# Attention and Fourier mixing on one core: 27 pairs of v loads change their issuing queue, from SyncE to ScalarE

## The chip, the cores and the metric

The kernel runs on one core of one Trainium2 chip. The metric is the device time in microseconds of one execution. A core has five engines that run side by side, each with an instruction queue of its own that is worked through in order: PE (TensorE, matrix products), DVE (VectorE), ACT (ScalarE), POOL (GpSimd) and SP (SyncE, which here only issues transfers). Transfers are issued by an instruction on one engine's queue, and the bytes are then moved by 16 DMA engines. An issue on SP is written SPq in the profile, one on ACT ACTq.

## What is computed

Top-k attention over 8 batches of 8 heads (576 rows, head size 64, the 32 largest scores of each row kept), whose output goes through a Fourier mixing, a normalisation and a two-layer network:

```python
scores = scale * np.matmul(q, k.transpose(0, 1, 3, 2))
kth = np.partition(scores, -top_k, axis=-1)[..., -top_k:-top_k + 1]
scores = np.where(scores >= kth, scores, -1e9)
attn = np.exp(scores - np.max(scores, axis=-1, keepdims=True))
attn = attn / (np.sum(attn, axis=-1, keepdims=True) + 1e-09)
out = np.matmul(attn, v)                        # (8, 8, 576, 64) -> x (8, 576, 512)
...
mixed = np.real(np.fft.fft(np.fft.fft(x, axis=1), axis=2))
u = x + mixed
un = (u - mu) / np.sqrt(var + 1e-06)
return u + np.maximum(un @ w_ch1, 0.0) @ w_ch2
```

All data are float32.

## The kernel before

**Work items.** Two heads make a pair (NPB = 4 pairs in a batch, 32 pairs), and a pair has nine items: five tiles of query rows, four of them once for each head. One step of the main loop (L1492) works on one item, so a batch is 36 steps and a pair nine. In step i the stages of several items run side by side: the scores of item i+3 (`scores`, PE, drained by ACT, L404, L375, L393), the search for the 32 largest of item i (`top_ops`, DVE, L425 and L427), the mask of item i-1 (`mask`: L448 on ACT, L451 on POOL), its exponential (`expo`, L459 on ACT), and for item i-2 the split of the weights into 16-bit halves (`plane`, two copies L472 on ACT), which SP writes to a scratch in HBM (L485, L488). `turn` (L506) reads the scratch back transposed into the tile PT, by a transposing transfer issued on SP. `attend` (L564) multiplies PT with v on PE, once for each of a pair's two chunks of rows: the first takes place a step after the transposition of the fifth item, the second after the ninth. This path through HBM is used by pairs from the second batch on, but for pairs 7 and 31; the others are transposed by PE (`transposes`).

**The mixing and the network.** Work of the batch before (`dft_tokens` L755, `dft_channels` L812 and L816, `channels_first` L881, and the network's `hidden` L966, `back` L993 and L1032, `fast` L1163) is cut into units, which the loop puts between the attention's matmuls so that PE is filled to an even level. Their results leave PSUM by ACT (L786, L833, L884, L970), in part with POOL (L839, L1108). In the first batch there is no such work; the weights of the network are converted instead.

**Order.** The order on every engine is that in which the program is written, a step after the other; nothing is rearranged. Transfers use eight completion semaphores in turn, whatever their queue, and a transfer waits until the one that had its semaphore before has landed.

**Loads.** At the end of a step the loop issues the loads of a coming pair: k in step 0 (L267, L271), q in step 5 (L240, L279), v in step 7 (L1599), all on SP. v has two tiles (L152), pair p in tile p % 2. `load_v` (L284) issues four transfers: for each of the two heads the first 512 rows (L288, 128 KB), and then, in `load_tails`, the last 64 rows (L255, 16 KB). Only the loads at the very start (L1271, L1275, L1277) are issued on ACT.

Of the kernel before, what the change touches and what calls it, by code (L numbers as in the profile page):

```python
# [73 lines left out]
def kernel(  # L74
# [9 lines left out]
    nc = tc.nc  # L84
# [11 lines left out]
    NPB = H // 2  # L96
# [129 lines left out]
    nat, qT_of, kT_of, v_of, PT, Ssb, Wk, Wp, M8, Nt = ({} for _ in range(10))  # L226
# [6 lines left out]
    def head_of(src, pair, e):  # L233
        b, hp = divmod(pair, NPB)
        return src[b, 2 * hp + e]
# [9 lines left out]
    def load_tails(dst, src, pair, queue=None, heads=(0, 1)):  # L245
        for e in heads:
            if src is q:
                for h in range(2):
                    (queue or nc.sync).dma_start(
                        out=dst[TH * h:TH * (h + 1), NF, e, :],  # L250
                        in_=head_of(src, pair, e)[HS * h + 2 * P:HS * (h + 1)],
                    )
            else:
                r0 = TAIL * e if src is v else 0
                (queue or nc.sync).dma_start(  # L255
                    out=dst[r0:r0 + TAIL, NF, e, :], in_=head_of(src, pair, e)[NF * P:S]
                )
# [26 lines left out]
    def load_v(pair):  # L284
        if pair < NPAIR:
            v_of[pair] = v_t[pair % 2]
            for e in range(2):
                nc.sync.dma_start(  # L288
                    out=v_of[pair][:, 0:NF, e, :],
                    in_=head_of(v, pair, e)[0:NF * P].rearrange("(c p) d -> p c d", p=P),  # L290
                )
            load_tails(v_of[pair], v, pair)

    def prep(n, pair, blocks=((0, NF), (NF, NC))):

# [1016 lines left out]
    for n in range(3):  # L1312
        load(n)
    load_v(0)
    load_nat("q", 1)
    for n in range(3, AHEAD):
# [123 lines left out]
    queue, waiting, pending, written, now, out_next = [], [], [], set(), [0], []  # L1440
    step_us = 6.0

    def chunk_at(i):

        for tile in (i - 4, i - 3, i - 2):
            r = tile % PER_PAIR
            if PER_BATCH <= tile < N and r in (4, 8):
                if i - tile == (4 if by_dma(tile) else 2 if tile == 2 * PER_BATCH - 1 else 3):
                    return tile // PER_PAIR, r // 8
        return None, None  # L1450
# [41 lines left out]
    while i < N + 5 or plan or queue or sums:  # L1492
# [49 lines left out]
        if short:  # L1542
            fixed += tok
            pair, r = divmod(i - 1, PER_PAIR)
# [39 lines left out]
        pair, ch = chunk_at(i)  # L1584
# [8 lines left out]
        if i < N:  # L1593
            if q_step:
                load_nat("k", pair_of + 1)
            if i % PER_PAIR == 5:
                load_nat("q", pair_of + 2)
            if i % PER_PAIR == 7:
                load_v(pair_of + 1)  # L1599
# [63 lines left out]
```

## Time and profile before

| | |
|---|---|
| median of 3 runs | 1876.23 us (1875.66 to 1876.6) |
| the profiled execution | 1876.57 us |
| its span on the core | 1874.8 us |
| mean granted clock of TensorE | 0.955 |
| SP's plain transfers of the planes, L485 and L488 | 260 issues |
| SP's transposing transfers, L506 | 130 issues, median 4.6 us from issue to landing |
| v's loads | 64 of 128 KB (3.0 us to landing) and 64 of 16 KB (2.5 us) |
| transfers in all | 249.16 MB, mean 133 GB/s |

The span is the time from the first to the last instruction of the profiled execution. "Busy" does not count issuing transfers or waiting for semaphores. In the page's slices the span is cut into 40 equal parts of some 47 us, and a digit is the busy share in tenths. The first batch ends after some 235 us; from the third batch on a batch takes about 205 us; the last batch's network runs alone from about 1703 us. In a row of the timeline the columns are the start, the duration, the engine, the line and operation, what is written and read, the number of instructions merged into the row, and in brackets the engine's idle time before it with what ended it.

### The profile page before, as it was taken

The page shows a single profiled execution, that of the slowest core. Times are in us where ns is not written, and L with a number is a line of the kernel's source. Part 1 is how long each engine was busy: PE and PEld are TensorE (multiplying, and loading weights), DVE is VectorE, ACT ScalarE, POOL GpSimd, SP SyncE. Part 2 cuts the span into 40 slices and gives each one's busy share as a digit, 9 for nine tenths or more (in the row PEclk, how much of TensorE's full clock was granted, in tenths as well). Part 3 has the DMA queues.
Part 4 walks back from the last instruction along what each step waited for, and adds up shares of the span by engine and source line. Part 5 has one row for each costly group of instructions (what it writes and reads, how often), then busy time and mean ns, then how long its engine had stood idle before and what let it go on. Part 6 is the DMA issues. An engine that isn't in the chain of part 4 may idle for free.

```text
span 1874.8 us, 26903 instructions
## 1 busy us (share of the span) xinstructions
PE 1703.8 (91%) x8134; PEld 1086.4 (58%) x8134; DVE 1583.8 (84%) x3301; ACT 1295.0 (69%) x3104; POOL 912.5 (49%) x1278
## 2 busy tenths in 40 slices
PE   5566699789899899999999999989999999999999
PEld 3344465355466555666556565666567555677677
DVE  7999989888899999999999899899999899762110
ACT  6878659577788788877787678767787678652100
POOL 4768643454746266355545465255545364341012
PEclk7777799999999999999999999999999999999999
DMA  5333016661557755586466745694566645530132
GB/s 167 104 98 109 20 46 170 168 164 26 137 146 202 187 130 136 150 209 161 123 161 180 180 114 132 155 231 127 122 162 182 172 121 143 130 111 6 51 114 69
DMA packets 516576, 249.16 MB, mean 133 GB/s; under 512 B 398288, under 2 KB 506448, under 8 KB 516432
## 3 DMA queue, kind: packets, MB, share of 16 engines
q1 hardware_dynamic: 515664, 247.23, 50.9%
q8 instruction: 65, 1.06, 0.2%
q14 instruction: 79, 0.65, 0.1%
q10 hardware_dynamic: 768, 0.21, 0.0%
HBM read 93.63 MB, written 84.74 MB: 95 GB/s over the span
## 4 chain that ended last, share of the span: by engine, by line
PE 55%; DVE 13%; ACT 10%; POOL 10%; issue 6%; DMA 4%; SPq 2%; POOLq 0%; DVEq 0%; ACTq 0%
PE hp L966 22%; PE o L564 7%; DVE wk L427 6%; DVE m L425 6%; PE sp L401 4%; PE cp L993 4%; POOL wk L451 4%; PE cw L1163 3%; PE cv L1163 3%; PE cp L1032 3%; ACT wk L448 2%; POOL fg L651 2%; PE yp L755 2%; ACT wk L472 2%; PE sp_t L371 2%
## 5 line engine op out<-in xcount | busy, mean ns | idle before, releaser
L451 POOL TENSOR_TENSOR wk<-S,wk 128x576 f32<-128x576 f32 x288 | 408.1, 1417 | 549.8 <-ACT wk L448 533.9
L425 DVE MAX8 m<-wk 128x8 f32<-128x576 f32 x864 | 626.5, 749 | 6.2
L966 PE MATMUL hp<-unT,w 128*128 128x256 f32 (+1 forms) x2048 | 529.5, 411 | 5.2 <-ACT unT L884 2.7
L966 PEld LDWEIGHTS hp<-unT,w 128*128 128x128 f32 x2048 | 382.5, 192 | 116.5 <-issue 10.7
L427 DVE MATCH_REPLACE8 wk<-m,wk 128x576 f32<-128x576 f32 x576 | 427.4, 742 | 0.0
L472 ACT COPY wk<-S 128x576 uint16<-128x576 uint16 x468 | 289.1, 668 | 0.0
L448 ACT ACTIVATE wk<-S,nt 128x576 f32<-128x576 f32 x288 | 222.9, 774 | 85.4 <-POOL nt L434 84.5
L564 PE MATMUL o<-PT,v 128*64 128x256 f32 (+3 forms) x1440 | 204.8, 430 | 37.9 <-DMA PT<-planes 19.5
L993 PE MATMUL cp<-w,hT 128*128 128x512 f32 x512 | 236.4, 602 | 0.0
L425 DVE MAX8 m<-S 128x8 f32<-128x576 f32 x288 | 213.5, 741 | 7.8 <-ACT S L375 7.8
L459 ACT ACTIVATE S<-wk,nt 128x576 f32<-128x576 f32 x234 | 184.2, 787 | 48.3 <-POOL wk L451 47.2
L427 DVE MATCH_REPLACE8 wk<-m,S 128x576 f32<-128x576 f32 x288 | 213.5, 741 | 0.0
L970 ACT ACTIVATE hT<-hp 128x320 f32<-128x320 f32 (+1 forms) x256 | 103.9, 412 | 156.3 <-PE hp L966 155.2
L401 PE MATMUL sp<-kT,qT 64*128 64x512 f32 (+1 forms) x528 | 170.7, 676 | 24.2 <-ACT kT L318 9.4
L564 PEld LDWEIGHTS o<-PT,v 128*64 128x64 f32 x1440 | 117.9, 158 | 114.9 <-issue 37.0
L404 ACT COPY S<-sp 128x512 f32<-128x512 f32 (+1 forms) x264 | 141.6, 586 | 24.4 <-PE sp L401 23.3
L993 PEld LDWEIGHTS cp<-w,hT 128*128 128x128 f32 x512 | 93.4, 193 | 91.4 <-issue 91.0
L1108 POOL TENSOR_TENSOR hT<-hT 128x512 f32<-128x512 f32 x64 | 81.6, 1277 | 106.5 <-ACT hT L970 91.5
L434 POOL TENSOR_TENSOR nt<-m,cc 128x2 f32<-128x2 f32 x288 | 59.1, 205 | 126.2 <-DVE m L425 122.5
L371 PEld LDWEIGHTS sp_t<-kt,qT 128*128 128x128 f32 x320 | 51.3, 196 | 108.9 <-issue 70.0
L1163 PE MATMUL cw<-w,hT 128*128 128x256 f32 x448 | 105.0, 381 | 1.5 <-POOL hT L1108 0.9
L527 PE MATMUL tpP<-ident,wk 128*128 128x128 f32 x216 | 40.8, 320 | 61.1 <-ACT wk L459 36.1
(160 smaller groups left out, 2174.3 us busy)
## 6 DMA issues: line engine op xcount, KB each, us to landing
planes<-wk SPq DMA_DIRECT2D x208, 288.0 KB, 2.7
w<-w_parts SPq DMA_DIRECT2D x82, 512.0 KB, 4.7
space<-in_moe_w_ch_dram SPq DMA_DIRECT2D x32, 512.0 KB, 3.7
nat<-in_q_dram SPq DMA_DIRECT2D x128, 64.0 KB, 2.7
v<-in_v_dram SPq DMA_DIRECT2D x64, 128.0 KB, 3.0
out_dram<-x SPq DMA_DIRECT2D x32, 256.0 KB, 2.7
nat<-in_k_dram SPq DMA_DIRECT2D x62, 128.0 KB, 3.0
planes<-wk SPq DMA_DIRECT2D x52, 144.0 KB, 2.6
```

Source lines behind the costliest of these rows:

```text
L401: nc.tensor.matmul(sp[r], lhsT=qT[hd, q_cols], rhs=kT[hd, :], start=True, stop=True)
L404: nc.scalar.copy(out=s_t[r, keys], in_=sp[r])
L425: ops.append(lambda src=src, m8=m8: nc.vector.max(out=m8, in_=src))
L427: ops.append(lambda src=src, m8=m8: nc.vector.match_replace(w, m8, src, NEG))
L448: nc.scalar.activation(out=w, in_=Ssb[i], func=AF.Relu, scale=-FAR, bias=Nt[i][:, 1:2])
L451: nc.gpsimd.tensor_tensor(out=w, in0=Ssb[i], in1=w, op=ALU.subtract)
L459: nc.scalar.activation(out=Ssb[i] if by_dma(i) else w, in_=w, func=AF.Exp, bias=Nt.pop(i)[:, 0:1], accum_out=den_t[pair % 3][:, c:c + 1],)
L472: nc.scalar.copy(out=words[:, half, :], in_=src[:, half, :])
L564: nc.tensor.matmul(o[D * e:D * (e + 1), c0:c1], lhsT=vv[:, c, e, :], rhs=pt[:, NF if c == NF else (NF + 1) * e + c, c0:c1], start=(c == 0) ...
L966: nc.tensor.matmul(hp[:, 0:w], lhsT=w1[:, dt, P * it:P * (it + 1)], rhs=unT[:, dt, 0:w], start=(dt == 0), stop=(dt == NDT - 1),)
L993: nc.tensor.matmul(cp, lhsT=hT[:, it, P * n:P * (n + 1)], rhs=w2[:, it, :], start=(it == 0), stop=(it == NIT - 1),)
L1163: nc.tensor.matmul(dst, lhsT=h()[a][:, kc, :], rhs=rhs_of(kc), start=start and kc == 0, stop=kc == NK - 1, skip_group_check=True,)
```

## The change

`load_v` chooses the queue by the number of the pair: SP for pairs 0 to 4, ACT for pairs 5 to 31. The place of the call in the program stays the same, the end of step 7, and so do the tiles, the sizes and the order of the four transfers.

```diff
     def load_v(pair):
         if pair < NPAIR:
             v_of[pair] = v_t[pair % 2]
+            queue = nc.sync if pair <= NPB else nc.scalar
             for e in range(2):
-                nc.sync.dma_start(
+                queue.dma_start(
                     out=v_of[pair][:, 0:NF, e, :],
                     in_=head_of(v, pair, e)[0:NF * P].rearrange("(c p) d -> p c d", p=P),
                 )
-            load_tails(v_of[pair], v, pair)
+            load_tails(v_of[pair], v, pair, queue)
```

`load_tails` had the argument for the queue already; without it, it uses SP. Pair 4 is the first of the second batch; as its load is issued in the first batch, it stays on SP.

## The prediction

> **What bounds the kernel now.** I read the page's busy times and slices first, then the windows view by batch, then the rows of v's loads, the waits, and the timeline around each load.
>
> ```profile
> PE 1703.8 (91%) x8134; PEld 1086.4 (58%) x8134; DVE 1583.8 (84%) x3301; ACT 1295.0 (69%) x3104; POOL 912.5 (49%) x1278
> ...
> PE   5566699789899899999999999989999999999999
> ...
> ACT  6878659577788788877787678767787678652100
> ```
>
> From about 480 us on PE is full and ACT is not. The windows view of two whole batches (PE, PEld, DVE, ACT, POOL busy, then clock, DMA share, GB/s) says how full:
>
> ```profile
> 896.00:1101.00 205.00, 199.03 (x962) 125.44 (x959) 192.02 (x398) 157.86 (x377) 105.39 (x157) 0.98 0.62 159
> ...
> 1311.00:1516.00 205.00, 198.68 (x964) 125.01 (x963) 191.46 (x397) 156.87 (x373) 104.63 (x154) 0.99 0.63 158
> ```
>
> PE 97% (199.03 / 205), DVE 94%, ACT 77%. So the price of anything put on ACT is what it makes PE wait. That is read place by place, since ACT drains every PSUM bank PE fills, in one fixed order.
>
> **What moves.** Pairs 5 to 31 are affected: 27 bursts of four issues (two of L288, two of L255), 108 in all. The same bytes go to the same tiles. The tile view of v gives the issue times on SP (min/median/max ns):
>
> ```profile
> L288 SPq DMA_DIRECT2D v<-in_v_dram x64: 419/570/1085, 8.0 to 1614.8; - x64
> L255 SPq DMA_DIRECT2D v<-in_v_dram x64: 513/595/794, 9.2 to 1616.0; - x64
> ```
>
> Four medians make 2 x 0.570 + 2 x 0.595 = 2.33 us. From the start of the first issue to the end of the fourth, the 27 bursts take a median of 2.53 us on SP, and I use that. In total 27 x 2.53 = 68 us leave SP and enter ACT's instruction order, where nothing behind a burst is dispatched until it is issued. Does an issue on ACT cost the same? The only rows are the first microseconds, when both queues issue at once:
>
> ```profile
> 0.74 0.97 SPq L240 DMA_DIRECT2D nat<-in_q_dram  x2
> 1.75 0.98 SPq L240 DMA_DIRECT2D kn<-in_k_dram  x2
> ```
> ```profile
> 0.74 0.41 ACTq L1271 DMA_DIRECT2D ident<-c_id  x1
> 1.19 1.09 ACTq L240 DMA_DIRECT2D kn<-in_k_dram  x2
> 2.32 0.54 ACTq L255 DMA_DIRECT2D kn<-in_k_dram  x1
> ```
>
> ACT takes 0.41 to 0.55 us an issue, SP 0.49, side by side. So the bounds of a burst on ACT are 4 x 0.41 = 1.64 us and, from the longest SP rows, 2 x 1.085 + 2 x 0.794 = 3.76 us. 2.53 is nearest to both queues' usual rows.
>
> **The waits that come with it.** Each load waits for the landing of an earlier transfer, normally the one eight back in the program's order, because eight completion semaphores go round. On ACT that could block the engine behind SP's queue. I compared, for each of the 108, the landing in this trace with the end of the ACT instruction ahead of the burst. Nearly all had landed 0.2 to 21 us before; the exceptions are the bursts at 1035.0 us (its fourth load's transposition lands at that moment) and at 1450.8 us (1.0 us later, but a fourth load starts some 1.9 us after the first). The wait for v's buffer is long over: its last reader ran four steps earlier. I cost these waits at nothing.
>
> **What lies behind a burst, and who waits.** Behind it on ACT stand the next step's mask (L448), the two half-word copies (L472), the score copies (L404, L375, L393) and the PSUM drains. L451 on POOL, SP's L485, and PE wait for these. I walked each place on the timeline: ACT becomes 2.53 us late; each idle gap of ACT takes off its length (not where it waited for POOL's L451, which is late too); at every matmul that waits for an ACT result, the stall is what is left of the lateness minus the matmul's own margin (its start minus that result's end). Two ends of the scale, first one of the two worst, the burst at 738.0 us, which goes after the first row:
>
> ```profile
> 737.88 0.20 ACT L459 ACTIVATION_READ_ACCUMULATOR S<-wk,nt 128x1 f32 x1
> 737.97 0.77 ACT L448 ACTIVATE wk<-S,nt 128x576 f32<-128x576 f32 x1
> ...
> 750.39 1.52 ACT L393 COPY S<-sp 64x256 f32<-64x256 f32 x4
> ...
> 751.19 2.84 PE L401 MATMUL sp<-kT,qT 64*128 64x512 f32 x4 [1.73 <-ACT S L393]
> ```
>
> ACT has only 0.2 us of gaps in these 13 us, and PE already waits for L393, with 0.05 us margin: it loses 2.3 us. The other end, at 1303.7:
>
> ```profile
> 1304.19 0.78 ACT L448 ACTIVATE wk<-S,nt 128x576 f32<-128x576 f32 x1 [0.48 <-POOL nt L434]
> ...
> 1314.26 0.43 ACT L786 COPY y<-yp 128x290 f32<-128x290 f32 x1 [2.53 <-PE yp L755]
> ```
>
> 0.48 + 2.53 us of gaps swallow it, and no matmul in between has a margin under 2.05 us. The cover here is ACT's wait for PE and DVE; without it, 2.5 us would be lost. Over the 27 places the stalls are: pair 7 2.4, pair 14 2.3, pair 17 1.3, pair 8 1.1, pairs 6, 22, 26 and 30 about 0.8 each, pairs 9 and 18 about 0.6 each, the other 17 none. Sum 11.7 us (rounding aside). With 1.64 us a burst the same walk gives 3.6 us, with 3.76 us it gives 31.2.
>
> Smaller terms. POOL is late with ACT, but of the matmuls that wait for POOL within 14 us of a burst only yp at 498 to 503 us has a margin under 2.5 us, and that stall is the same time as pair 9's above: nothing more. Transfers: v on a queue of its own shares the 16 engines with the transposition that SP has just issued, instead of standing behind it, and for ten pairs the first attend starts within 0.2 us of that landing. A burst is 2 x 128 + 2 x 16 = 288 KB, 1.8 us at the window's 159 GB/s if all of it stood in the way: 0 to 18 us, and as the transposition is ahead I take 2. Against these, PE time lost is not lost twice where PE later waits for something else: it idles some 53 us between 480 and 1700 us in this trace. I take 3 off (bounds 0 and all 11.7). Sum: 11.7 + 2 - 3, about +11 us on the profiled execution's 1876.57 us, which is 0.3 us over the median: 1887.
>
> **What SP gets back.**
>
> ```profile
> 738.47 1.22 SPq L288 DMA_DIRECT2D v<-in_v_dram  x2
> 739.74 1.33 SPq L255 DMA_DIRECT2D v<-in_v_dram  x2
> 741.17 0.60 SPq L485 DMA_DIRECT2D planes<-wk  x1
> ```
>
> At 14 of 27 bursts the next SP transfer starts within 0.11 us of the last v issue, so v held it up. But that L485 waits for L472 copies which now stand behind the burst on ACT. Here they end at 739.9 and would end at 742.4, later than the 741.17 at which L485 starts now. I credit nothing.
>
> [...]
>
> **The rivals.** That the moved loads would not move is no rival: the built program has all 108 on ACT.
> - *Forecast (0.56).* +11 us, 1887. Its own range is the walk's two ends with the small terms, 1880 to 1908.
> - *Hidden (0.20).* A burst counts 1.64 us, because its issue overlaps the ACT work ahead, and later PE waits take back what is left of the 3.6: 0 to +3 us, about 1878. For: 17 of 27 places lose nothing even at 2.53. Against: the row ahead of a burst is mostly the accumulator read of 0.2 us, which covers little.
> - *Issues collide (0.10).* A burst meets one of SP's transposition issues (L506, median 2.48 us) and waits it out: 2.53 + 2.48 = 5.0 us late at each place, for which the same walk gives about 59 us, 1936. For: one of them is often in progress within 2 us of a burst. Against: the side-by-side rows.
> - *SP's queue was the brake (0.14), the other side.* Planes and transpositions go out up to 2.53 us sooner and PE stops waiting for PT. The tile view of o has PE's idle time ahead of attend (us, times):
>
> ```profile
>   DMA PT<-planes: 22.8, 7
> ```
>
> All of it gone would be 1854; half of it, 11 us, gives 1865. It decides if PE's second attend of a pair, whose transpositions SP issues after v, is the one that waits. For: the 14 places. Against: of the second attends only one (615.9 us, 4.7 us) starts at its landing, the others have 0.7 us or more; the first attend's transpositions are issued ahead of v.
>
> **How the numbers follow.** What a measurement of this kernel can tell from no change is about 0.2%, 3.75 us: 1872.5 to 1880. The hidden case is "same", 0.20; the brake case is "faster", 0.14; the forecast and the collision are "slower", 0.56 + 0.10 = 0.66. The range 1870 to 1910 holds the forecast's and the hidden case's; it leaves out most of the brake case (0.09) and the collision (0.10).
>
> **What the new profile would show.** Right: 27 groups of four ACTq rows for v, 2.3 to 2.8 us each, the fourth with no gap for a wait; more time in PE's waits for ACT (sp <- L393 is 8.1 us between 480 and 1703 us now) at the places named, most at 751 us and after the bursts of pairs 22, 26 and 30; SP's L485 after the old v slot no earlier than now by more than a few tenths. Wrong: single ACTq rows of 2 us or more (collision, or a blocked semaphore); PE waits for ACT unchanged (hidden); the 22.8 us of PT waits clearly smaller (brake). The forecast falls also if the first attends start 1 us or more later after the burst than their margin allows, since I took nearly nothing for the shared transfer engines.

## The result, and the profile after

The changed kernel takes 1886.78 us (median of four runs, 1883.47 to 1888.17), the kernel before beside it 1875.96 (1875.66 to 1876.6). The ratio is 1.0055, 95% interval 1.0037 to 1.0072: slower by some 10 us, 7 to 14 by the interval. The profiled execution took 1888.17 us, with a span of 1886.3 us and a mean granted clock of 0.948 (0.955 before).

The page's busy times and slices of the changed kernel:

```profile
PE 1715.3 (91%) x8134; PEld 1093.6 (58%) x8134; DVE 1584.0 (84%) x3301; ACT 1293.2 (69%) x3104; POOL 911.6 (48%) x1278
...
PE   6567699789899999999999999999999899999999
...
ACT  6878658666787777777787678767787678652100
```

PE still bounds the kernel and is as full as before. It executes the same 8134 matmuls, but is busy 11.5 us longer (1715.3 against 1703.8), while its idle time over the whole span, the span less the busy time, is 171.0 us in both. So either matmuls became slower, or "busy" holds something that isn't work. This is taken up below.

The windows of two whole batches, the same two as before (the columns are the window's length, then busy us of PE, PEld, DVE, ACT, POOL, then clock, DMA share and GB/s):

```profile
905.00:1110.00 205.00, 197.87 (x963) 125.03 (x960) 191.74 (x398) 156.62 (x376) 104.55 (x156) 0.98 0.62 158
1320.00:1526.00 206.00, 197.50 (x962) 125.02 (x962) 190.83 (x396) 155.50 (x374) 103.76 (x155) 0.98 0.62 158
```

One batch is as long as before, the other 1.7 us longer by the lag at its two ends. The lag of a matmul is how much later than in the kernel before it starts. It goes up and down in steps: +4.9 us at 464 us, +2.7 at 643, +8.6 at 844, +10.2 at 1046, +8.7 at 1171, +11.6 at 1601. Some of what is lost is given back where PE has another wait anyway.

v's loads in the tile view (min/median/max ns):

```profile
L289 ACTq DMA_DIRECT2D v<-in_v_dram x54: 368/466/722, 283.8 to 1630.2; - x54
L255 ACTq DMA_DIRECT2D v<-in_v_dram x54: 472/607/1517, 285.0 to 1631.4; - x54
```

All 108 are on ACT, and a row costs about what it cost on SP (medians 466 and 607 ns, 570 and 595 there). A burst, from the start of the first row to the end of the fourth, has a median of 2.21 us (2.14 to 3.05). The timeline of ACT around one burst (columns as in the timelines above):

```profile
1311.83 0.38 ACT L971 ACTIVATE hT<-hp 128x256 f32<-128x256 f32 x1 [1.20 <-PE hp L967]
1311.84 0.93 ACTq L289 DMA_DIRECT2D v<-in_v_dram  x2
1312.81 1.17 ACTq L255 DMA_DIRECT2D v<-in_v_dram  x2
1314.09 0.78 ACT L449 ACTIVATE wk<-S,nt 128x576 f32<-128x576 f32 x1 [1.87 <-DMA v<-in_v_dram]
```

The first issue starts at 1311.84, while L971 runs until 1312.21: here ACT's queue issues a transfer 0.37 us before the instruction ahead of it ends. So the burst of 2.14 us leaves a hole of 1.87 us, in which ACT computes nothing. Over the 27 bursts the hole has a median of 1.82 us (0.89 to 2.59), 45.0 us in all. That is the number that the prediction's 2.53 stood for. The holes of 0.89 to 1.05 us stand where several ACT instructions ahead of the burst still ran while it was issued (the loads of pairs 5, 14, 18, 22, 26 and 30); there the first issue starts some 1.4 us before the last of them ends.

PE's waits from 480 us to the last attend, first before, then after (us in total, times, longest):

```profile
PE o L564 <- DMA PT<-planes: 10.4, 3, 4.7
PE o L564 <- DVE m L425: 9.3, 3, 4.3
PE sp L401 <- ACT S L393: 8.1, 6, 2.1
PE sp L401 <- ACT kT L318: 5.1, 5, 1.2
PE o L564 <- DVE x L1121: 4.5, 2, 2.8
```
```profile
PE o L565 <- DMA PT<-planes: 13.5, 5, 6.5
PE o L565 <- DVE m L426: 9.6, 3, 4.7
PE sp L402 <- ACT S L394: 9.0, 6, 2.6
PE sp L402 <- ACT kT L319: 5.9, 5, 1.4
...
PE o L565 <- DMA v<-in_v_dram: 3.5, 2, 3.2
PE o L565 <- DVE wk L428: 3.1, 1, 3.1
```

The waits for ACT grew by 0.9 and 0.8 us only. The waits of the attends (the rows with o; some are put down to a DVE instruction, though an attend reads nothing of DVE's, only PT and v, which transfers bring) went from 10.4 + 9.3 + 4.5 = 24.2 us to 13.5 + 9.6 + 3.5 + 3.1 = 29.7 us.

A load on ACT did not wait for an issue on SP here. The burst for pair 6 goes out within one of SP's transposing issues, which lasts 7.82 us, and its four rows are as short as elsewhere (timeline of ACT, then of SP):

```profile
329.07 1.13 ACTq L289 DMA_DIRECT2D v<-in_v_dram  x2
...
330.25 1.36 ACTq L255 DMA_DIRECT2D v<-in_v_dram  x2
```
```profile
324.21 7.82 SPq L507 DMA_TRANSPOSE PT<-planes  x1
```

SP, relieved of 68 us of issues, waits for ACT instead. In the waits of its queue the row of the planes goes from the first of these lines (before) to the second (after):

```profile
SPq L485 <- ACT wk L472: 352.1, 112, 15.4
```
```profile
SPq L486 <- ACT wk L473: 427.8, 129, 15.4
```

**Where 11.5 us of busy time come from.** One attend shows it: pair 23's first. Timeline of PE before, then after:

```profile
1249.52 0.49 PE L371 MATMUL sp_t<-kt,qT 128*128 128x128 f32 x2
1251.63 2.91 PE L564 MATMUL o<-PT,v 128*64 128x320 f32 x20 [1.62 <-DVE x L1121]
```
```profile
1258.26 0.49 PE L372 MATMUL sp_t<-kt,qT 128*128 128x128 f32 x2
1261.94 4.34 PE L565 MATMUL o<-PT,v 128*64 128x320 f32 x20 [3.19 <-DMA v<-in_v_dram]
```

PE waits 1.62 us before and 3.19 after; the same 20 matmuls then take 2.91 and 4.34 us. (The brackets name DVE and a load of v, but the v that this attend reads had landed by 1210.15 us. What lands last is the pair's third transposition, at 1261.69 us, 8.39 us after its issue began; v's first issue follows that by 1.50 us. Before, v's followed by 4.73 us, and the transposition took 6.74 us.) The windows view gives the clock over those matmuls, before and after (the last three numbers: granted clock, DMA share, GB/s):

```profile
1252.00:1256.00 4.00, 4.00 (x27) 2.67 (x24) 3.97 (x10) 2.50 (x7) 1.61 (x2) 1.00 0.91 248
```
```profile
1261.90:1264.90 3.00, 2.96 (x12) 1.65 (x14) 2.97 (x8) 1.03 (x2) 1.58 (x2) 0.51 0.73 241
```

Behind the longer wait the clock is halved for 3.4 us. The wait cost 1.57 us more, the slow attend another 1.43 us. (Here both are given back: some 10 us later the kernel before waits 2.4 us for a weight, the changed one doesn't, and the lag is 8.7 us again, as it was ahead of the attend.) Adding up the clock's records from 240 us on, the profiled execution of the kernel before has 64.9 us at half clock in 13 stretches, that of the changed one 92.2 in 19, each 3.4 or 6.8 us long. If work goes at half speed in them, 27.3 us more are worth up to 13.7 us of PE's time, an estimate from the granted share (0.51 in the window above).

That the idle time over the whole span is the same is chance. The window from 240 us, before the first moved load, to the end, in the kernel before, then in the changed one:

```profile
240.00:1874.80 1634.80, 1551.53 (x7389) 994.36 (x7385) 1357.68 (x2826) 1109.92 (x2672) 750.71 (x1105) 0.98 0.54 138
```
```profile
240.00:1886.30 1646.30, 1558.10 (x7377) 998.28 (x7373) 1358.18 (x2821) 1108.20 (x2672) 749.10 (x1105) 0.97 0.53 137
```

Up to 240 us, where nothing has moved yet, PE is idle 4.9 us less in the changed kernel's execution (82.8 against 87.7), and from there on 5.0 us more (88.2 against 83.3). From the first moved load to the end the same matmuls take 13.1 us longer, 5.0 of them idle and 8.2 busy. So in these two executions the stalls are the smaller part of the loss, and PE running slower behind them is the larger.

How long a wait must be for the clock to be halved behind it isn't shown: 2.09 us at 1158.2 us in the kernel before was followed by 6.8 us at half clock, while 2.84 us at 838.6 was followed by none.

### The profile page after: what moved, and what is told of

It reads as the page before. It is cut to its first block, busy times and chain, and to the rows that moved or that the text cites. A ratio compares the mean times of both kernels' runs of the same rounds, so it can differ in the third digit from the quotient of the medians.

```text
span 1886.3 us, 26881 instructions
## 1 busy us (share of the span) xinstructions
PE 1715.3 (91%) x8134; PEld 1093.6 (58%) x8134; DVE 1584.0 (84%) x3301; ACT 1293.2 (69%) x3104; POOL 911.6 (48%) x1278
## 4 chain that ended last, share of the span: by engine, by line
PE 56%; ACT 10%; DVE 10%; POOL 10%; issue 5%; DMA 5%; SPq 2%; ACTq 1%; POOLq 0%; DVEq 0%
PE hp L967 22%; PE o L565 7%; DVE m L426 4%; PE sp L402 4%; DVE wk L428 4%; PE cp L994 4%; POOL wk L452 4%; PE cw L1164 3%; PE cp L1033 3%; PE cv L1164 3%; ACT wk L449 2%; PE yp L756 2%; ACT wk L473 2%; POOL fg L652 2%; DMA planes<-wk 2%
## 5 line engine op out<-in xcount | busy, mean ns | idle before, releaser
L565 PE MATMUL o<-PT,v 128*64 128x256 f32 (+3 forms) x1440 | 210.6, 439 | 44.2 <-DMA PT<-planes 25.1
L971 ACT ACTIVATE hT<-hp 128x320 f32<-128x320 f32 (+1 forms) x256 | 103.4, 411 | 150.0 <-PE hp L967 149.0
L402 PE MATMUL sp<-kT,qT 64*128 64x512 f32 (+1 forms) x528 | 174.7, 692 | 24.6 <-ACT S L394 9.2
L405 ACT COPY S<-sp 128x512 f32<-128x512 f32 (+1 forms) x264 | 141.4, 584 | 24.0 <-PE sp L402 21.3
L435 POOL TENSOR_TENSOR nt<-m,cc 128x2 f32<-128x2 f32 x288 | 58.3, 202 | 87.5 <-DVE m L426 82.8
L402 PEld LDWEIGHTS sp<-kT,qT 64*128 64x128 f32 (+1 forms) x528 | 47.5, 196 | 83.8 <-issue 31.0
```

What stands on the lines that cost most here:

```text
L402: nc.tensor.matmul(sp[r], lhsT=qT[hd, q_cols], rhs=kT[hd, :], start=True, stop=True)
L405: nc.scalar.copy(out=s_t[r, keys], in_=sp[r])
L565: nc.tensor.matmul(o[D * e:D * (e + 1), c0:c1], lhsT=vv[:, c, e, :], rhs=pt[:, NF if c == NF else (NF + 1) * e + c, c0:c1], start=(c == 0) ...
```

## The experiments

Each ratio is against the kernel before, run beside it on the same chip, with its 95% interval; 0.1% is 1.9 us. A single profiled execution stands some us beside its kernel's median, so that numbers from one trace show places, and the ratios show prices.

### Hold and load taken apart

What is asked first is whether the hold of ACT costs the 10 us, or v's way through another queue. Four kernels: v's loads left out, ACT held without moving v, both, and half of the burst moved.

`no_v`, v's loads of pairs 5 to 31 left out:

```diff
     def load_v(pair):
         if pair < NPAIR:
             v_of[pair] = v_t[pair % 2]
+            if pair > NPB:
+                return
```

> The loads of v for pairs 5 to 31 are left out (attend multiplies with the v of pairs 3 and 4), so neither SP nor ACT issues them. Theory 'hold' (the change costs because ACT is held while it issues; SP gets nothing back): as the kernel before, 0.998 to 1.001, since 68 us of issues on SP lie beside other work. Rival 'brake' (SP's issues of v hold up planes and transpositions): faster, 0.994 or less. Rival 'queue' (the loss comes from v's transfers running beside the transpositions on a queue of their own): 0.998 to 1.001 as well.

Measured: 1870.82 us against 1877.44, ratio 0.9968 (0.9956 to 0.9979).

`sp_hold`, the loads on SP as before, and ACT held by four copies at the same places. The copies stood on ACT for 1.90 us at every place (51 us in all), next to the burst's hole of 1.82 (45 us in all):

```diff
+    held = const.tile([P, 344], U16, name="held", tag="held")
+
+    def hold():
+        for _ in range(4):
+            nc.scalar.copy(out=held, in_=w1[:, 0, 0:172].bitcast(U16))
...
             if i % PER_PAIR == 7:
                 load_v(pair_of + 1)
+                if NPB < pair_of + 1 < NPAIR:
+                    hold()
```

> v stays on SP as in the kernel before; at the place where the change put the burst on ACT, ACT does four copies of 128x344 16-bit words onto a scratch instead, about 1.9 us, for the same 27 pairs. Theory 'hold': slower like the change, 1.004 to 1.007, with the granted clock at half for some 20 to 30 us more than before after 240 us. Rival 'queue': 0.999 to 1.001, since no transfer moved. Rival 'semaphores' (SP's later transfers wait for the landing of a v load that ACT issues late): 0.999 to 1.001.

Measured: 1884.03 us, ratio 1.0033 (1.0021 to 1.0045).

`no_v_hold`, both edits together:

> Both: v's loads for pairs 5 to 31 are left out and ACT is held for about 1.9 us at their 27 places. Theory 'hold': the same as sp_hold within 0.2%, 1.003 to 1.007. Rival 'queue': as no_v, 0.998 to 1.001. If SP's relief and ACT's hold both counted, this would lie clearly under sp_hold.

Measured: 1876.13 us, ratio 0.9995 (0.9980 to 1.0010).

`half`, the two 128 KB loads of a burst on ACT, the two tails on SP:

```diff
-            load_tails(v_of[pair], v, pair, queue)
+            load_tails(v_of[pair], v, pair)
```

> The change with one part undone: the two loads of 128 KB are issued on ACT, the two of 16 KB stay on SP. 256 of a burst's 288 KB still run on ACT's queue, but ACT is held for some 0.4 us (0.9 us of issues less the 0.4 to 0.8 us by which a burst starts before the ACT instruction ahead of it ends). Theory 'hold': the walk gives under 1 us, so 0.999 to 1.002. Rival 'queue': most of the loss stays, 1.004 to 1.006.

Measured: 1883.31 us, ratio 1.0026 (1.0014 to 1.0038).

None of the four met the ranges of theory 'hold': `no_v` is faster than it allows, `no_v_hold` lies in its rival's range, `sp_hold` lies just under it, and `half` lies between it and its rival.

What follows: at step 7 the hold costs 0.33% with v on SP, and 0.9995 - 0.9968 = 0.27% with no v at all, so it is a price of its own, 5 to 6 us, wherever v goes. The change costs 0.55%, so 0.22% are left for v's way, with an uncertainty of some 0.2% from the two intervals. `half` shows better that such a second part exists: its two issues mostly run under the instruction ahead and leave ACT without work for 0.32 us on average while they go out (8.7 us in all, against 40.6 us for the change counted the same way), and yet it loses 0.26%. At the price of `sp_hold`, 6.2 us for 51, 8.7 us would be worth 1.1 us, 0.06%. The tile view of o in `half` has these rows of PE's and ACT's idle time ahead of the attends:

```profile
  DVE m L426: 29.5, 10
  DMA PT<-planes: 27.7, 8
  DVE wk L428: 18.2, 7
```

Before, the rows that answer were 21.3, 22.8 and 1.4 us (and 13.3 for another DVE row, which `half` doesn't have): 58.8 us then, 75.4 in `half`. From 480 us on the waits of PE ahead of the attends are 24.2 us before, 23.3 in `sp_hold`, 29.6 in `half` and 29.7 in the changed kernel. So in these traces the attends wait longer where v goes out on ACT, and not where ACT is only held. Whether these waits are the loss is another question, to which the last group of runs below has an answer.

### One step later

`act_s8` keeps the changed kernel's queue and moves the place from step 7 to step 8; `sp_s8` moves the place alone, on SP.

```diff
-            if i % PER_PAIR == 7:
+            if i % PER_PAIR == (7 if pair_of < NPB else 8):
                 load_v(pair_of + 1)
```

> The changed kernel with v's burst on ACT's queue one step later from the second batch on: step 8 of a pair instead of 7. At step 7 the pair's third transposition (t = 4) has just been issued and chunk 0's attend of the same pair waits for it; at step 8 that attend stands ahead of the burst and no transposition is issued in the step. Theory 'two parts' (ACT held about 0.3%; v on a queue of its own slows the transposition beside it, and the attends of pairs 10, 15, 19, 23 and 27 wait longer for it, about 0.25%): the second part goes, ratio 1.002 to 1.004, 1880 to 1885 us at a before of 1877, and the lag at those five attends against the kernel before grows by less than 0.5 us each. Rival 'the queue's semaphores or the issues alone cost it, wherever they stand': ratio 1.005 to 1.007 as in the changed kernel. Rival 'the hold alone': 1.005 too, as the hold is the same, or another number if step 8 takes a hold better or worse.

Measured: 1878.65 us against 1877.73, ratio 1.0002 (0.9986 to 1.0018). Neither number expected: the loss is gone, the hold's part too. The lag at the five attends named, counted from the matmul ahead of each, grows by 0.10, 2.17, 1.43, 0.41 and 2.59 us, where less than 0.5 was expected (in the changed kernel by 1.22, 0.94, 0.78, 1.56 and 2.25). So these attends start as late as in the changed kernel, and yet the kernel is no slower.

> The kernel before with v's four loads still on SP's queue but at step 8 of a pair instead of 7 from the second batch on. Theory 'v's transfer beside the third transposition costs the before kernel something too' (leaving v out gained 0.3%): ratio 0.997 to 0.999. Rival 'on SP the loads queue behind the transposition anyway and what leaving v out gained is SP's issue time, which is the same at step 8': 0.999 to 1.002.

Measured: 1875.18 us, ratio 0.9990 (0.9978 to 1.0002). It lies between the two expectations, and isn't told from no change.

`hold_s8` is `sp_hold` with the four copies one step later and v at step 7 on SP:

```diff
-                if NPB < pair_of + 1 < NPAIR:
-                    hold()
+            if i % PER_PAIR == 8 and NPB < pair_of + 1 < NPAIR:
+                hold()
```

> The kernel before with v on SP's queue at step 7, as it was, and ACT held at the end of step 8 instead of step 7 by the same four copies (some 1.9 us, 27 places). The step 7 hold cost 0.33%, and the burst on ACT at step 8 (v moved there too) cost 0.02%. Theory 'a hold costs by the slack of the transpositions and copies behind it, about the same at both steps' (walking the slack of the before trace with 1.84 us at each place gives 5.0 us at step 7 and 6.4 us at step 8): ratio 1.002 to 1.004, and v's later place gained what hid it. Rival 'step 8 has the slack for it': 0.999 to 1.001, and the change would have cost nothing one step later for that reason.

Measured: 1880.40 us against 1878.62, ratio 1.0013 (1.0003 to 1.0024), between the two theories. The same 1.90 us on ACT cost 0.33% at step 7 and 0.13% at step 8. Together with v's place, -0.10%, that is +0.03%, and `act_s8` has +0.02%; but each of these three is known to 0.1 or 0.16% only, so that they neither show nor exclude a part for the queue as such at step 8. The walk of the slack, which gave 5.0 us for step 7 (measured 6.2) and 6.4 for step 8 (measured 2.5), doesn't foresee the difference between steps.

The copies also stand for more than v's burst at step 8. There more ACT instructions stand just ahead of the burst, and the queue issues under all of them (timeline of ACT in `act_s8`, the burst for pair 23):

```profile
1202.28 1.07 ACT L405 COPY S<-sp 128x512 f32<-128x512 f32 x2
1202.78 1.04 ACTq L289 DMA_DIRECT2D v<-in_v_dram  x2
...
1203.86 0.69 ACTq L255 DMA_DIRECT2D v<-in_v_dram  x1
1204.12 0.23 ACT L460 ACTIVATION_READ_ACCUMULATOR S<-wk,nt 128x1 f32 x1
1204.59 0.61 ACTq L255 DMA_DIRECT2D v<-in_v_dram  x1
1205.25 0.78 ACT L449 ACTIVATE wk<-S,nt 128x576 f32<-128x576 f32 x1 [0.90 <-POOL nt L435]
```

The burst begins 1.57 us before the last of them ends, and the hole is 0.90 us, which is also the median of the 27 places at step 8 (34.8 us in all), against 1.82 at step 7 (45.0 us in all). So the change costs nothing that can be measured one step later, ACT is held for less there at most places, and a hold of the same length costs less there too; how much each of these gives isn't shown.

`act_s8` also has in full what the prediction looked for in the changed kernel, issues on ACT that wait for another transfer (timeline of ACT):

```profile
1040.31 0.52 ACTq L289 DMA_DIRECT2D v<-in_v_dram  x1
...
1041.31 0.22 ACT L460 ACTIVATION_READ_ACCUMULATOR S<-wk,nt 128x1 f32 x1
1041.51 2.04 ACTq L255 DMA_DIRECT2D v<-in_v_dram  x2
1043.60 0.77 ACT L449 ACTIVATE wk<-S,nt 128x576 f32<-128x576 f32 x1 [2.07 <-DMA w<-w_parts]
```

The third issue starts 0.02 us after one weight load lands (1041.49), the fourth 0.02 us after the next (1043.06), and ACT stands for 2.07 us. A wait of this kind happens at three of the 27 places (pairs 16, 20 and 28 of the loads). In the changed kernel, where the same loads go out at step 7, it happens once: the fourth issue of pair 28's burst waits 0.53 us, to 1460.54, for a transposition that lands at 1460.52.

### Which of the 27 places cost

A theory from the two traces: SP issues a pair's third transposition only after its planes have landed (in all, its queue waits for planes 107 times ahead of L506 in the kernel before, 204.3 us); ACT doesn't wait for that. In the kernel before, v's first issue always comes 2.0 us or more after the start of that transposition's issue. In the changed kernel it comes ahead of it at seven places (pairs 5, 10, 15, 17, 19, 27 and 29). Pair 19, timeline of SP in the changed kernel (v goes out on ACT from 1043.62 to 1046.02):

```profile
1042.51 1.23 SPq L489 DMA_DIRECT2D planes<-wk  x2
1043.84 1.16 SPq L910 DMA_DIRECT2D w<-w_parts  x2
1046.25 1.31 SPq L507 DMA_TRANSPOSE PT<-planes  x1
```

The transposition that chunk 0's attend waits for starts 2.6 us after v's first issue; the planes ahead of it take 3.05 us to land (2.48 at the same place before), the transposition 5.88 (5.58 before). The three kernels that were made to try this put v on ACT at the eight places alone where it goes first or the transposition landed latest (`only8`: the loads of pairs 6, 11, 16, 18, 20, 24, 28 and 30), at the 19 others alone (`other19`), and on SP but ahead of the transposition at all 27 (`sp_early`).

```diff
-            queue = nc.sync if pair <= NPB else nc.scalar
+            queue = nc.scalar if pair in (6, 11, 16, 18, 20, 24, 28, 30) else nc.sync
```

> The kernel before with v on ACT's queue in 8 of the 27 places alone: where, in the trace of the changed kernel, the burst was issued before the third transposition of the pair it stands in (pairs 5, 10, 15, 17, 19, 27, 29: 0.1 to 7.3 us before it) or that transposition landed latest (pair 23: 8.4 us). Theory 'overtaking' (SP waits for the planes' landing before it issues that transposition, ACT doesn't wait, so v's 295 KB go first and chunk 0's attend, which TensorE already waits for in these pairs, gets its PT later): most of the loss is in these 8, ratio 1.003 to 1.005 (5 to 9 us), 0.6 us or more of lag at the attends of pairs 10, 15, 19, 23 and 27. Rival 'the loss is spread evenly, by ACT's hold at every place': 8/27 of 0.55%, ratio 1.001 to 1.002.

Measured: 1881.26 us against 1877.83, ratio 1.0013 (0.9998 to 1.0028).

> The complement: v on ACT's queue in the 19 other places, on SP's in those 8. Theory 'overtaking': ratio 1.000 to 1.0025 (0 to 5 us, what ACT's hold costs where the transposition is first). Rival 'spread evenly': 19/27 of 0.55%, ratio 1.003 to 1.0045.

Measured: 1886.29 us, ratio 1.0043 (1.0030 to 1.0057).

`sp_early`:

```diff
+        if i < N and i % PER_PAIR == 7 and pair_of >= NPB:
+            load_v(pair_of + 1)
         turn(i - 3)
...
-            if i % PER_PAIR == 7:
+            if i % PER_PAIR == 7 and pair_of < NPB:
                 load_v(pair_of + 1)
```

> The kernel before with v's four loads still on SP's queue, but issued at the start of step 7, ahead of the third transposition instead of behind it (from the second batch on). ACT isn't held at all and no second queue is used. Theory 'overtaking': v's bytes are again ahead of the transposition, at all 27 places, and SP's 2.1 us of issues too where the planes have landed by then: slower, ratio 1.002 to 1.006, with lag at the attends of pairs 10, 15, 19, 23 and 27. Rival 'a queue of its own on ACT is what costs, not the order': 0.999 to 1.001.

Measured: 1881.44 us, ratio 1.0015 (1.0001 to 1.0029).

The theory that the loss sits in those eight places falls: they cost 0.13%, the 19 others 0.43%, and the sum, 0.56%, is the whole change. Per place that is as good as even (0.016% and 0.023%). Order by itself isn't free, though: `sp_early`, with no hold and no second queue, has v ahead of the transposition everywhere and loses 0.15%, just told from nothing and in neither of its two ranges.

What the order does is seen in the traces, one of each kernel. Over the 26 first attends the lag that is added right at the attend, summed, is 10.9 us in the changed kernel, 11.6 in `half`, 9.3 in `only8`, 10.7 in `sp_early` and 8.3 in `act_s8`, but 1.9 in `other19`, 1.5 in `sp_hold`, 1.0 in `hold_s8` and 0.2 in `sp_s8`. So the overtaking theory is right about these waits: the eight places make nearly all of them. It is wrong about the time: `only8` has the waits and costs 0.13%, `other19` has hardly any and costs 0.43%. By these prices, most of what is lost at these attends is given back behind them, as at pair 23 above. The third transposition itself, from issue to landing, takes 99.1 us in sum over the 26 pairs before and 99 to 101 in the traces with v on SP at step 7 or 8 or left out, and 104 to 111 in the six traces that have v on ACT; `act_s8` has 105.6 of them and loses nothing, so this isn't the price either.

### The clock behind the waits

Idle matmuls, whose result nothing reads, ahead of eight attends that wait, in the kernel before and in the changed one:

```diff
+    FILL = {(4, 0): 6, (5, 0): 10, (10, 0): 6, (10, 1): 10, (15, 0): 6,
+            (19, 0): 8, (23, 0): 6, (27, 0): 8}
...
         o = o_of[pair, ch]
+        for _ in range(FILL.get((pair, ch), 0)):
+            nc.tensor.matmul(
+                o[:, DM - P:DM], lhsT=ident, rhs=ident, start=True, stop=True
+            )
```

> The kernel before with idle matmuls (128x128 of the identity into columns of o's bank that nothing reads) ahead of eight attends that wait for a transposition: pairs 4, 5, 10, 15, 19, 23, 27 chunk 0 and pair 10 chunk 1; 6 to 10 each, 0.27 us each by the 128-column attends, shorter than the waits. Theory 'a wait of over about 2 us is paid twice, as TensorE's granted clock is halved for 3.4 or 6.8 us behind it': the halved stretches at 335, 615, 1041 and 1458 us go or shrink, half-clock time after 240 us falls from 65 us by 10 to 24 us, and the time falls by half of that, ratio 0.993 to 0.998. Rival 'the halved clock costs nothing, as the work behind it isn't the bound, or the fill doesn't hold the clock': 0.999 to 1.002.

Measured: 1874.24 us against 1877.73, ratio 0.9980 (0.9966 to 0.9993). Half-clock time fell from 64.9 to 47.8 us, by 17.1. Pair 19's attend on PE, before and with the idle matmuls:

```profile
1037.69 0.49 PE L371 MATMUL sp_t<-kt,qT 128*128 128x128 f32 x2
1042.06 5.60 PE L564 MATMUL o<-PT,v 128*64 128x320 f32 x20 [3.88 <-DMA PT<-planes]
```
```profile
1037.98 1.95 PE L566 MATMUL o<-ident 128*128 128x128 f32 x16
1042.12 4.49 PE L571 MATMUL o<-PT,v 128*64 128x320 f32 x20 [2.19 <-issue]
```

The attend starts at the same moment, as its transposition lands when it lands, and is done 1.0 us sooner.

> The changed kernel with the same idle matmuls ahead of the same eight attends. Theory 'much of the change's loss is the halved clock behind the longer waits of those attends': half-clock time after 240 us falls from 92 us to 60 to 70 us, and the time falls by 10 to 15 us, ratio 0.998 to 1.001 against the kernel before; the difference between the two kernels with fill is then about the hold's alone, 0.2 to 0.4%. Rival 'the waits themselves are the loss': ratio 1.004 to 1.007, no change from the changed kernel.

Measured: 1886.37 us, ratio 1.0041 (1.0026 to 1.0056). Half-clock time fell from 92.2 to 68.3 us. The time fell by some 0.14 of the 0.55%, on another chip than the changed kernel's own run and inside both intervals, so less than the theory wanted and at the rival's lower end.

So in the kernel before, waits of PE at these attends are paid a second time through the clock: the eight fills take 17.1 us off the time at half clock and gain 0.20%. But 17 us at half clock would be worth 8.5 us of work by the estimate above, and the gain is 3.5 us. The sums of half-clock time also move by themselves: `sp_s8` has 81.9 us of it and is no slower than before, `sp_hold` has 68.3 and is slower by 0.33%. So the 27.3 us between the two kernels can't be booked as a cause.

`before_fill` beats both kernels: the kernel before by 0.20%, and the changed one by some 0.75% if the two ratios are set side by side. Together with v at step 8 it wasn't run.

## Why the prediction was right in its sum and where its steps were wrong

Forecast +11 us, 1887.0; measured 1886.78, +10.8 by the medians. Step by step:

- **Where the price comes from.** "The price of anything put on ACT is what it makes PE wait": half right. The hold of ACT is 0.33% of the 0.55; another part comes nearly without a hold (`half`). "ACT drains every PSUM bank" holds for most of them only: DVE reads some of cp, cv, cw, mp and tpx (L608, L822, L1008, L1121).
- **The burst, 2.53 us.** Mis-sized: ACT's hole is 1.82 us. A burst is a bit shorter on ACT (2.21 us), and its start lies under the instruction ahead. The hidden rival named that overlap; the argument against it, that the row ahead is "mostly the accumulator read of 0.2 us", was wrong, as the queue ran ahead of the read and of the instruction before it too (the first issue starts 0.20 to 1.51 us before the last instruction ahead ends).
- **The stalls, 11.7 us.** Too much: `sp_hold` measures 6.2 us (3.9 to 8.4), and that is net of what later waits take back, so it stands against 11.7 - 3 = 8.7. The same walk with 1.84 us gives 5.0 before anything is taken back. That is nearer, but the walk missed step 8 (6.4 against 2.5), so its being near at step 7 may be luck. At the places the profile has, as growth of the lag at matmuls that wait for ACT: pair 7 1.8 us at the waits (2.4 foreseen), pair 8 0.7 (1.1), pair 14 0.9 (2.3), pair 17 0.8 (1.3); at 22, 26 and 30 nothing of the 0.8 each. That is 4.2 us in all; the walk looked only at matmuls that wait for an ACT result, and the larger steps in this trace, 10.9 us, stand at the first attends, which wait for a transposition. At pair 14 POOL held the next mask back by itself for part of the hole, so that the waiting score matmul went from 1.73 us to:

```profile
756.98 2.83 PE L402 MATMUL sp<-kT,qT 64*128 64x512 f32 x4 [2.60 <-ACT S L394]
```

- **v on a queue of its own, +2 us.** The other mis-sized term: 0.22% by difference and 0.26% by `half`, 4 to 5 us, within the bounds 0 to 18. The reason "the transposition is ahead" held at 19 of 26 places only. That isn't the mechanism alone, since the places where v goes first cost no more than the others. What is shown: with v on ACT at step 7 this part exists (`half`), and at step 8, where the third transposition is 5.6 us old (median) when v starts, the whole move costs 0.02%. What carries it isn't shown; the longer waits of the first attends and the longer third transpositions are there in `act_s8` too, which is no slower.
- **-3 us for lateness that later waits swallow.** Not measured by itself, since every run's time is net of it. That it happens is seen in the trace: the lag falls by 2.9 us at 1265 us.
- **SP gets back nothing.** Right: the planes' wait for ACT grew by 75.7 us where SP issued 68 us less. The brake rival fell with it. `no_v` is 6 us faster than the kernel before, but that takes the bytes away too.
- **Semaphores at nothing, collisions.** Right for the change: the longest row is 1.517 us, one of 108, and one issue waits 0.53 us, in the burst that the prediction named as doubtful (1450.8 us there). One step later such waits are longer, as `act_s8` showed. The 16 rows on ACT that lie mostly within one of SP's transposing issues have a median of 0.52 us, the 92 others 0.53 (pair 6's burst is shown above), so the collision rival falls.
- **What the new profile would show.** 27 groups on ACT: yes, 12 of them at 2.3 us or more and 15 below. More wait for ACT: barely, 0.9 us, which was the sign set down for the hidden case. PT waits over the whole tile view: 22.8 to 29.9 us, no brake. The sign that came true most was the last one, longer waits of first attends: 1 us or more at several of them, for example 2.25 us at 1469 us. By its own words the forecast's account falls with that, though its number stood.

So the sum was right by luck: two errors stood against each other, the hold's net 8.7 us too large by some 2.5, and v's 2 us too small by 2 to 3.

## What to carry to other kernels

What the loads cost ACT when they moved to its queue was the hole they left (1.82 us, median), not the burst (2.21): in another kernel, see from the timeline how far the queue runs ahead at that very place. A walk of the slack with that hole is an estimate only; here it missed the difference between two steps. Such a move also leaves the order that the old queue kept without anyone writing it down (here v overtook the third transposition at seven of 27 places), and here a price came even where the engine was hardly held (0.26% in `half`, with 0.32 us a place). Try the same move one step later before judging the queue, since here that took the cost from 0.55% to 0.02%. Don't read the price off the waits that grew: put the change at some of the places alone and time that, since here the places with the longer waits were the cheaper ones. Where the bound engine is TensorE, look at the granted clock behind its waits, since here a wait was paid for once more: behind one of 3.19 us, at pair 23, the clock was 0.51, and 20 matmuls took 4.34 us instead of 2.91.

## What was not expected of the hardware

- From 240 us on, a stretch of 3.4 or 6.8 us with a granted clock of 0.5 begins within, or up to 1.5 us behind, 13 of the 20 PE waits of 1.7 us or more in the kernel before and all 17 in the changed one. Idle matmuls in the waits made such time less, from 64.9 to 47.8 us in the kernel before: at pair 19's attend 20 matmuls went from 5.60 us to 4.49, and the stretch at half clock there from 6.8 us to 3.4.
- A transfer's issue on ACT's queue started before the instructions ahead of it ended: the first issue of a burst by 0.20 to 1.51 us before the last of them ends in the changed kernel, and by up to 1.80 in `act_s8`. So four issues left a hole of 1.82 us at step 7 and of 0.90 at step 8 (medians).
- Issues on ACT stood still until loads on SP's queue had landed, and ACT with them: 2.07 us at 1041.5 us in `act_s8`.
